# State reads head by head, in two column halves of TensorE, with the column sums directly behind

## The chip, the cores and the metric

The kernel runs on one core of a Trainium2 chip. The core has engines with a queue of instructions each: TensorE (PE) multiplies matrices, VectorE (DVE), ScalarE (ACT) and GpSimd (POOL) work on tiles element by element, SyncE (SP) issues DMAs. SBUF is the working memory with 128 partitions; PSUM takes TensorE's results in eight banks. The metric is the time of one execution on the device in microseconds (us), the median of several runs; lower is better.

A matmul of TensorE has a stationary operand, the weights, which a separate instruction (LDWEIGHTS, row PEld of the profile) loads into the array, and a moving operand that streams through it. In the profile "128\*64 128x32" would be weights of 128 rows and 64 columns, and a moving operand of 128 partitions and 32 columns.

## The reference

Inputs are `x` (8 batches, 8 heads, 512 tokens, 64 features), `state` (8, 8, 32, 64) and the weights of a feed-forward layer. For each batch and head:

```
scores = x @ state^T / 8            # 512 x 32
xread  = softmax over the 32 states  of scores   @ state    # 512 x 64
sread  = softmax over the 512 tokens of scores^T @ x        #  32 x 64
rows   = concat(xread, sread)       # 544 rows a batch, heads side by side: 512 columns
h = rows @ w_in; g = h + sin(alpha*h)^2/alpha; out = g @ w_out
```

The change concerns `sread`, the state reads: for each head, the sum over tokens of exp(score) times x, and its denominator, the sum over tokens of exp(score).

## The kernel before

Each batch has 512 tokens in four chunks of 128 (`C` = 4), and eight heads as four pairs (`Q` = 4), two pairs to a group (`G` = 2). `E` holds the exponentials of a batch: 128 tokens by group, chunk, and 128 columns, which are two pairs by two heads by 32 states (`Ns`). `xp` holds x with tokens on the partitions: chunk, head, 64 features.

The order of all instructions is written out by hand in the list `ORDER` (line 21 on): each word is a step with its arguments, and since every engine works through its own instructions in that order, the list sets each engine's queue. The steps that matter here:

- `sc`, `ex` (scores, exponentials of a group), `rs`, `rr`, `nm`, `ad` (the softmax over states and its transposed copy).
- `w.b.bank` (line 445): the reads of batch b. For each pair and chunk, one matmul with both heads of x as weights (128 tokens x 128 columns) and both heads' exponentials moving (64 columns). The four chunks accumulate in PSUM. The result has heads (even features, odd features) on the partitions and (even states, odd states) on the columns; only the two diagonal blocks, even with even and odd with odd, are used by anybody.
- `cs.b` (line 456): the denominators. Weights are a tile of ones, 128 x 64; for each chunk one matmul for the even heads into PSUM partitions 0 to 63 and one for the odd heads into 64 to 127, 128 moving columns each, into the last third of the same PSUM tile. `half(r)` (line 203) is the slice of 64 partitions.
- `rc.b` (line 466): DVE takes the reciprocal of the sums. `xs.b.r` (line 470): DVE multiplies the block of parity r on partition half r with it, and writes `xs_all`, which the feed-forward of "batch 8", all state rows together, uses late.
- `m` (line 478): the state times w_in for a later batch, in matmuls with 64 x 32 weights.
- `h`, `si`, `sq`, `gt`, `o`, `oc`, `os`: the feed-forward in 16 slices of 128 hidden columns. `h` (line 537) and `o` (line 587) are the bulk of TensorE's work, with 128 x 128 weights and 512 moving columns.

In the list `w.0`, `w.2` and `w.4` stand some steps ahead of their `cs`, with o or h steps between. `cs.0` and `cs.2` stand directly before an `m` as TensorE sees it. `w.1`, `w.3`, `w.6`, `w.7` are followed by their `cs` with no other TensorE work between. `w.5` comes before `w.7`, and `cs.5` directly behind `cs.7`.

Of the kernel before, what the change touches and what calls it, by code (L numbers as in the profile page):

```python
# [56 lines left out]
o.1.1.4.7 sq.1.11.A pk.3.0.V sq.1.14.G o.1.1.7.8 gt.1.10 td.3 o.1.2.8.9 sc.2.0.0 o.1.1.8.9 gt.1.11  # L57
o.1.1.9.10 ex.2.0 o.1.3.0.2.6 gt.1.14 o.1.3.2.4 o.1.2.9.10 o.1.3.4.5 o.1.2.10.12 ex.2.1 o.1.2.12.13
rs.2.0 o.1.1.10.11 m.2.2.2.4.3.0 rr.2.0 rs.2.1 o.1.2.13.14 nm.2.0.0.4.G me.2.3.0.A o.1.2.14.15 w.0.1
rr.2.1 me.2.2.1.A me.2.3.1.V o.1.3.5.6 nm.2.1.0.4.G me.2.2.0.A o.1.3.6.7 o.1.2.15.16 cs.0 oc.1.2.A  # L60
m.2.0.3.4.0.2 ad.2 rc.0 o.1.3.7.8 me.2.1.1.A o.1.3.8.9 sc.3.0.7 xs.0.1 me.2.1.0.A o.1.1.11.12 os.1.2
me.2.0.0.V sc.3.1.2 me.2.0.1.A o.1.1.12.13 o.1.3.9.10 xs.0.0 o.1.3.10.11 ex.3.0 o.1.1.13.16 ex.3.1
rs.3.0 o.1.3.11.13 oc.1.1.A o.1.3.13.14 rr.3.0 h.2.0.0 rs.3.1 nm.3.0.0.4.G os.1.1 o.1.3.14.16 si.2.0
# [28 lines left out]
sq.4.1.G gt.4.2 o.3.3.12.13 h.4.13.6 si.4.3 gt.4.15 o.3.3.13.15 si.4.13 sq.4.3.G o.3.3.15.16 gt.4.1  # L92
h.4.6.5 oc.3.3.A o.3.2.12.13 h.4.5.1 sq.4.13.G si.4.6 gt.4.3 os.3.3 h.4.14.2 si.4.5 o.3.0.0.1.4
sq.4.6.G o.3.2.13.14 gt.4.13 si.4.14 o.3.0.1.4 sq.4.5.A h.4.4.0 sq.4.14.G gt.4.6 o.3.0.4.5 h.4.0.6
si.4.4 gt.4.5 o.3.1.4.6 si.4.0 sq.4.4.G gt.4.14 o.3.2.14.16 w.2.5 sq.4.0.A pk.6.1.V o.3.1.6.7
oc.3.2.A h.4.7.1 pk.6.0.V gt.4.4 sc.5.0.2 td.6 si.4.7 o.3.1.7.8 sc.5.1.7 gt.4.0 o.3.1.8.9 o.3.0.5.6
ex.5.0 sq.4.7.G o.3.0.6.8 o.3.1.9.11 os.3.2 o.3.0.8.9 gt.4.7 o.3.0.9.12 cs.2 ex.5.1 rs.5.0
m.5.0.0.6.1.2 o.3.0.12.13 rr.5.0 me.5.0.0.A rs.5.1 o.4.3.0.1.7 nm.5.0.0.4.G o.3.0.13.14 me.5.0.1.A
o.3.0.14.15 rr.5.1 o.3.1.11.12 me.5.1.1.V o.3.1.12.13 me.5.1.0.A nm.5.1.0.4.G o.4.3.1.3 rc.2
o.3.0.15.16 o.4.3.3.4 o.3.1.13.14 oc.3.0.A ad.5 o.3.1.14.15 xs.2.0 m.6.0.0.6.2.1 xs.2.1 o.4.3.4.5  # L100
me.6.1.1.V me.6.1.0.A sc.6.1.4 os.3.0 sc.6.0.5 me.6.0.1.A o.4.3.5.6 me.6.0.0.V o.4.3.6.7 ex.6.0
o.4.3.7.8 o.4.0.0.1.2 o.3.1.15.16 ex.6.1 rs.6.0 w.3.1 oc.3.1.A cs.3 rr.6.0 m.5.2.6.0.5.4 rs.6.1
nm.6.0.0.4.G os.3.1 o.4.3.8.9 me.5.2.0.A me.5.2.1.V o.4.0.1.2 o.4.3.9.10 me.5.3.0.A o.4.3.10.11
rr.6.1 o.4.2.0.1.3 rc.3 nm.6.1.0.4.G o.4.2.1.2 me.5.3.1.A h.5.8.6 o.4.3.11.12 xs.3.1 h.5.9.0 si.5.8
ad.6 xs.3.0 o.4.0.2.3 o.4.3.12.14 o.4.2.2.4 h.5.4.5 si.5.9 o.4.3.14.15 sq.5.8.V h.5.3.4 si.5.4
gt.5.8 o.4.2.4.5 sq.5.9.G h.5.0.1 si.5.3 o.4.3.15.16 o.4.0.3.4 si.5.0 sq.5.4.G o.4.2.5.6 oc.4.3.V
o.4.2.6.8 sq.5.3.A gt.5.9 h.5.1.6 os.4.3 sq.5.0.G h.5.5.7 gt.5.4 si.5.1 o.4.2.8.10 si.5.5 gt.5.3
h.5.2.0 sq.5.1.G o.4.2.10.11 gt.5.0 o.4.2.11.12 si.5.2 h.5.14.5 lx.7.0.1 sq.5.5.A gt.5.1 h.6.3.4
o.4.2.12.13 si.5.14 gt.5.5 o.4.2.13.14 sq.5.2.G o.4.0.4.5 o.5.0.0.1.1 si.6.3 o.4.2.14.15 h.6.6.6
sq.5.14.A sq.6.3.G gt.5.2 o.4.0.5.6 h.5.13.7 si.6.6 gt.5.14 o.4.0.6.8 si.5.13 sq.6.6.G o.4.0.8.9  # L110
gt.6.3 o.4.0.9.11 sq.5.13.A o.4.0.11.12 h.6.2.0 gt.6.6 h.5.12.5 si.6.2 gt.5.13 o.4.2.15.16 h.6.4.4
si.5.12 sq.6.2.G o.4.0.12.13 oc.4.2.V o.4.0.13.14 si.6.4 o.4.0.14.15 o.4.1.0.1.6 os.4.2 o.4.1.1.2
sq.5.12.A gt.6.2 sq.6.4.G o.5.0.1.3 o.4.0.15.16 gt.5.12 h.5.10.7 oc.4.0.A o.4.1.2.3 gt.6.4 o.4.1.3.4
si.5.10 o.4.1.4.5 os.4.0 o.4.1.5.6 pk.7.1.V o.4.1.6.7 sq.5.10.A o.4.1.7.8 pk.7.0.V o.4.1.8.10 td.7
gt.5.10 m.6.2.3.0.5.2 o.4.1.10.11 me.6.3.0.V me.6.3.1.A o.4.1.11.12 h.5.7.4 me.6.2.1.A me.6.2.0.V
h.5.11.7 si.5.7 h.5.15.2 si.5.11 h.5.6.5 sq.5.7.V h.6.15.0 si.5.15 gt.5.7 sq.5.11.G o.4.1.12.13
o.5.2.0.1.3 si.5.6 o.5.2.1.3 si.6.15 sq.5.15.G o.4.1.13.14 gt.5.11 o.4.1.14.16 sq.5.6.A h.6.11.4
sq.6.15.G oc.4.1.V h.6.1.7 si.6.11 gt.5.15 o.5.2.3.4 os.4.1 h.6.0.6 si.6.1 sq.6.11.G gt.5.6
o.5.0.3.5 si.6.0 o.5.0.5.6 w.4.2 sq.6.1.A gt.6.15 sq.6.0.G o.5.0.6.7 gt.6.11 o.5.0.7.8 o.5.2.4.5
sc.7.1.5 gt.6.1 sc.7.0.0 o.5.2.5.7 ex.7.0 gt.6.0 o.5.0.8.10 o.5.2.7.8 o.5.1.0.2.4 o.5.0.10.11  # L120
h.6.14.7 ex.7.1 h.6.13.6 rs.7.0 cs.4 si.6.14 rs.7.1 o.5.1.2.4 o.5.0.11.12 rr.7.1 o.5.0.12.13 rc.4
o.5.2.8.9 nm.7.1.0.4.G h.6.10.0 o.5.0.13.14 si.6.13 xs.4.1 o.5.2.9.10 sq.6.14.G o.5.2.10.11 xs.4.0
si.6.10 o.5.2.11.13 h.6.7.5 sq.6.13.A rr.7.0 nm.7.0.0.4.G o.5.2.13.15 si.6.7 h.6.12.2 sq.6.10.A
gt.6.14 gt.6.13 o.5.1.4.5 ad.7 sq.6.7.G o.5.1.5.7 si.6.12 gt.6.10 o.5.1.7.10 sq.6.12.A gt.6.7
o.5.1.10.11 o.5.0.14.15 o.5.1.11.12 gt.6.12 o.5.0.15.16 h.6.5.7 oc.5.0.A o.6.2.0.1.6 h.6.9.0 si.6.5
os.5.0 o.5.2.15.16 o.5.1.12.13 si.6.9 sq.6.5.V o.5.1.13.14 o.6.2.1.2 oc.5.2.V o.5.3.0.1.5 sq.6.9.A
o.6.2.2.3 o.5.3.1.2 gt.6.5 os.5.2 o.6.2.3.5 o.5.3.2.3 gt.6.9 o.5.3.3.7 m.7.2.2.1.3.7 o.5.1.14.15
me.7.3.0.A me.7.3.1.V o.6.2.5.7 me.7.2.0.A o.6.2.7.8 me.7.2.1.V w.6.0 cs.6 m.7.0.3.7.2.1 rc.6
o.5.3.7.8 me.7.1.0.A o.5.3.8.10 me.7.0.1.V me.7.0.0.A o.5.3.10.11 h.6.8.2 me.7.1.1.A xs.6.0
o.5.3.11.12 xs.6.1 h.7.11.3 si.6.8 o.5.3.12.13 h.7.7.7 si.7.11 sq.6.8.V o.5.1.15.16 gt.6.8 w.5.1  # L130
si.7.7 sq.7.11.G o.5.3.13.14 oc.5.1.A o.6.3.0.1.0 o.5.3.14.15 sq.7.7.A o.5.3.15.16 gt.7.11 os.5.1
h.7.0.2 oc.5.3.A w.7.4 gt.7.7 si.7.0 cs.7 os.5.3 cs.5 h.7.5.3 rc.7 sq.7.0.A o.6.3.1.3 si.7.5
h.7.15.5 xs.7.0 xs.7.1 o.6.3.3.4 sq.7.5.A rc.5 o.6.3.4.6 o.6.2.8.9 si.7.15 o.6.2.9.11 gt.7.5
o.6.3.6.7 sq.7.15.A o.6.3.7.8 h.7.3.7 gt.7.0 o.6.3.8.9 h.7.14.4 si.7.3 gt.7.15 h.7.8.3 si.7.14
xs.5.0 sq.7.3.G h.7.6.2 xs.5.1 si.7.8 o.6.3.9.10 o.6.2.11.13 sq.7.14.G si.7.6 gt.7.3 o.6.2.13.16
# [22 lines left out]
class Steps:  # L158
# [245 lines left out]
    def ex(k, b, g):  # L404
        E = k.new(b, "E", k.epool, [k.P, k.G, k.C, k.P], BF16)
        k.nc.scalar.activation(E[:, g], k.t["sc", b, g][:], ACT.Exp, scale=k.scale)  # L406

    def rs(k, b, g):
        R = k.new(b, "R", k.smallp, [k.P, k.G, k.C * 4], FP32)
        k.nc.vector.reduce_sum(  # L410
            R[:, g], k.t["E", b][:, g].rearrange("p c (h j) -> p (c h) j", j=k.Ns), axis=AX.X
        )
# [5 lines left out]
    def nm(k, b, g, c0, c1, eng):  # L418
        A = k.new(b, "A", k.apool, [k.P, k.G, k.C, k.P], BF16)
        n = (c1 - c0) * 2  # L420
        a = A[:, g, c0:c1].rearrange("p c (e r j) -> p (c e) r j", r=2, j=k.Ns)
        e = k.t["E", b][:, g, c0:c1].rearrange("p c (e r j) -> p (c e) r j", r=2, j=k.Ns)
        rb = k.t["rR", b][:, g, c0 * 4:c1 * 4].rearrange("p (e r) -> p e r", r=2)
# [20 lines left out]

    def w(k, b, bank):
        wc = k.t["w", b] = k.ps(bank, [k.P, k.Q, 3 * k.Ns], FP32, "w_ps")
        E = k.t["E", b]
        for q in range(k.Q):
            for i in range(k.C):
                k.nc.tensor.matmul(  # L450
                    wc[:, q, 0:2 * k.Ns], k.pair(b, i, q),
                    E[:, q // 2, i, (q % 2) * 2 * k.Ns:(q % 2 + 1) * 2 * k.Ns],
                    start=(i == 0), stop=(i == k.C - 1),
                )

    def cs(k, b):
        E, wc = k.t["E", b], k.t["w", b]
        for i in range(k.C):
            for r in range(2):
                Ev = E[:, :, i, :].rearrange("p g (h r j) -> p g h r j", h=2, r=2)  # L460
                k.nc.tensor.matmul(  # L461
                    wc[k.half(r), :, 2 * k.Ns:], k.ones[:], Ev[:, :, :, r],
                    start=(i == 0), stop=(i == k.C - 1),
                )
# [199 lines left out]
```

The softmax here doesn't subtract the row's maximum and nothing guards it: scores larger than these inputs give would overflow.

## Time and profile before

| | us |
|---|---|
| median of 3 runs (221.13 to 221.43) | 221.16 |
| span of the profiled execution | 221.2 |
| TensorE busy | 215.7 |
| ScalarE busy | 173.5 |
| VectorE busy | 162.4 |
| GpSimd busy | 107.1 |
| reads `w` (line 450), 128 matmuls, busy | 5.0 |
| sums `cs` (line 461), 64 matmuls, busy | 3.1 |
| `m` (line 488), 256 matmuls, busy | 10.2 |

TensorE's granted clock is shown as full for the whole span. Busy times of TensorE overlap each other at their ends, because a matmul's length as shown includes the tail in which the next one already runs. What a matmul costs in a stream is the distance from its start to the next one's. "idle before <-issue" on a row of PEld is time in which the weight loader waited for nothing that the profile shows. The trace holds every start to a nanosecond; its views print hundredths of a microsecond.

### The profile page before, as it was taken

How to read it: one execution, taken by the hardware profiler on the slowest of the kernel's cores; microseconds unless marked ns; L12 is line 12 of the kernel's file. 1: busy time of each engine (PE TensorE's matmuls, PEld its weight loads, DVE VectorE, ACT ScalarE, POOL GpSimd, SP SyncE). 2: the span in 40 equal slices, each digit the busy share in tenths (PEclk: the TensorE clock that was granted, in tenths of full speed). 3: DMA queues.
4: the chain of work that ended last, by engine and by line, in shares of the span. 5: the costliest groups of instructions: out<-in, count | busy, mean ns of one | idle time of the engine just before them, and what ended most of it. 6: DMA issues, size and time to landing. Idle time of an engine off the chain costs nothing.

```text
span 221.2 us, 4330 instructions
## 1 busy us (share of the span) xinstructions
PE 215.7 (97%) x1619; PEld 106.0 (48%) x1619; DVE 162.4 (73%) x286; ACT 173.5 (78%) x297; POOL 107.1 (48%) x115
## 2 busy tenths in 40 slices
PE   7999999999999999999999999999999999999994
PEld 3664454444444444444454444445445555665452
DVE  3468986999678979988888778889766988571201
ACT  3589878998899979998996999798857897685111
POOL 6866626595388728934863377363501072121000
PEclk9999999999999999999999999999999999999999
DMA  6999995953549518375325437380220211012042
GB/s 172 198 206 204 205 203 87 174 199 73 119 127 158 96 50 150 44 190 61 81 41 125 126 95 94 108 117 17 47 99 0 98 47 47 0 50 95 1 142 96
DMA packets 38052, 23.48 MB, mean 106 GB/s; under 512 B 20992, under 2 KB 33680, under 8 KB 38032
## 3 DMA queue, kind: packets, MB, share of 16 engines
q0 software_dynamic: 11648, 8.13, 26.1%
q1 hardware_dynamic: 26128, 15.08, 26.1%
q8 instruction: 12, 0.20, 0.4%
q14 instruction: 8, 0.07, 0.1%
q10 hardware_dynamic: 256, 0.01, 0.1%
HBM read 17.44 MB, written 8.91 MB: 119 GB/s over the span
## 4 chain that ended last, share of the span: by engine, by line
PE 93%; ACT 3%; DMA 2%; SPq 0%; issue 0%
PE o_ps L587 54%; PE h_ps L537 22%; PE m_ps L488 4%; PE h_ps L543 3%; PE h_ps L552 3%; DMA x<-in_x_dram 2%; PE s_ps L399 2%; PE warm_ps L303 2%; PE w_ps L450 2%; PE w_ps L461 1%; PE x_ps L361 1%; ACT L226 1%; ACT s L560 1%; ACT M L496 1%; PE x_ps L376 0%; PE st_ps L333 0%
## 5 line engine op out<-in xcount | busy, mean ns | idle before, releaser
L587 PE MATMUL o_ps<-w_out_sb,gT 128*128 128x512 bf16 (+2 forms) x560 | 137.7, 373 | 0.0
L576 DVE SCALAR_TENSOR_TENSOR gT<-s,inva_sb,h_ps 128x512 bf16<-128x512 bf16 (+1 forms) x144 | 96.6, 714 | 18.8 <-POOL s L201 9.6
L201 POOL TENSOR_TENSOR s<-s 128x512 bf16<-128x512 bf16 (+1 forms) x76 | 76.7, 1021 | 65.9 <-ACT s L560 62.4
L560 ACT ACTIVATE s<-h_ps,alpha_sb 128x512 bf16<-128x512 f32 (+1 forms) x144 | 88.8, 671 | 10.5 <-PE h_ps L543 4.3
L587 PEld LDWEIGHTS <-gT 128*128 128x128 bf16 x560 | 52.3, 98 | 60.3 <-issue 5.0
L537 PE MATMUL h_ps<-AT,M 128*128 128x512 bf16 x224 | 60.8, 379 | 0.0
L537 PEld LDWEIGHTS <-M 128*128 128x128 bf16 x224 | 21.7, 98 | 25.9 <-issue 0.4
L569 ACT ACTIVATE s<-s 128x512 bf16<-128x512 bf16 (+1 forms) x53 | 31.4, 595 | 0.8
L201 POOL TENSOR_TENSOR A<-E,rR 128x512 bf16<-128x512 bf16 x16 | 16.6, 1048 | 25.7 <-ACT o_sb L595 12.7
L595 ACT COPY o_sb<-o_ps 128x512 f32<-128x512 f32 (+2 forms) x24 | 13.7, 571 | 16.6 <-PE o_ps L587 16.5
L496 ACT CAST M<-m_ps 128x512 bf16<-128x512 f32 x35 | 18.6, 594 | 8.2 <-PE m_ps L488 8.1
L496 DVE CAST M<-m_ps 128x512 bf16<-128x512 f32 x29 | 18.9, 679 | 2.5 <-PE m_ps L488 2.1
L595 DVE COPY o_sb<-o_ps 128x512 f32<-128x512 f32 x11 | 7.6, 691 | 13.0 <-PE o_ps L587 12.9
L303 PE MATMUL warm_ps<-warm 128*128 128x128 bf16 (+3 forms) x66 | 9.9, 295 | 1.4 <-DVE warm L209 1.2
L410 DVE TENSOR_REDUCE R<-E 128x16 f32<-128x512 bf16 x16 | 10.4, 658 | 1.1 <-ACT E L406 0.9
L201 DVE TENSOR_TENSOR s<-s 128x512 bf16<-128x512 bf16 (+1 forms) x15 | 6.2, 415 | 6.8 <-ACT s L560 6.7
L488 PE MATMUL m_ps<-w_in_sb,stT 64*32 64x512 bf16 x256 | 10.2, 382 | 0.0
L468 DVE RECIPROCAL rC<-w_ps 128x128 f32<-128x128 f32 x8 | 7.6, 948 | 3.2 <-PE w_ps L461 3.2
L406 ACT ACTIVATE E<-s_ps 128x512 bf16<-128x512 f32 x16 | 8.8, 601 | 1.4 <-PE s_ps L399 1.3
L552 PE MATMUL h_ps<-AT,M 128*128 128x512 bf16 x32 | 9.4, 380 | 0.4 <-ACT M L496 0.4
L543 PE MATMUL h_ps<-xs_all,w_in_sb 128*128 128x256 bf16 x64 | 9.1, 273 | 0.0
L560 ACT ACT_TABLE_LOAD x5 | 6.4, 1283 | 2.2 <-PE h_ps L537 1.1
(56 smaller groups left out, 104.3 us busy)
## 6 DMA issues: line engine op xcount, KB each, us to landing
out_dram<-o_sb SPq DMA_DIRECT2D x33, 256.0 KB, 2.3
xnat<-in_x_dram POOLq DMA_DIRECT2D x7, 512.0 KB, 7.7
w_in_sb<-in_moe_w_in_dram POOLq DMA_DIRECT2D x4, 512.0 KB, 10.3
w_out_sb<-in_moe_w_out_dram POOLq DMA_DIRECT2D x4, 512.0 KB, 16.3
x<-in_x_dram SPq DMA_DIRECT2D x4, 256.0 KB, 4.3
st_nat<-in_state_dram POOLq DMA_DIRECT2D x1, 256.0 KB, 5.7
out_dram<-o_sb SPq DMA_DIRECT2D x1, 192.0 KB, 1.9
s<-in_state_dram SPq DMA_DIRECT2D x1, 128.0 KB, 2.1
```

What stands on the lines that cost most here:

```text
L201: {"V": k.nc.vector, "G": k.nc.gpsimd}[eng].tensor_tensor(out, a, b, ALU.mult)
L303: k.nc.tensor.matmul(wp[:, :cols], k.warm[:, 0:k.P], k.warm[:, :cols], start=True, stop=True)
L488: k.nc.tensor.matmul(k.t["m", b, s + n, g][o0:o0 + k.Ns, :], k.stT[k.half(r), b * k.G + g, c0:c0 + k.Ns], k.w_in_sb[k.half(r), 2 * g + h, ...
L496: k.copy(eng)(k.t["M", b][:, g, s * k.FW:(s + 1) * k.FW], k.t["m", b, s, g][:])
L537: k.nc.tensor.matmul(hp[:, :n], k.t["M", t][:, g, fs], k.t["AT", t][:, g, :], start=(g == 0), stop=(g == k.G - 1),)
L543: k.nc.tensor.matmul(hp[:, :n], k.w_in_sb[:, q, fs], k.xs_all[:, q].rearrange("p b j -> p (b j)"), start=(q == 0), stop=(q == k.Q - 1),)
L552: k.nc.tensor.matmul(k.t["h", t, f][:], k.t["M", t][:, g, f * k.P:(f + 1) * k.P], k.t["AT", t][:, g, :], start=(g == 0), stop=(g == k.G - 1),)
L560: k.nc.scalar.activation(s[:, :n], k.t["h", t, f][:, :n], ACT.Sin, scale=k.alpha_sb[:, f:f + 1])
L569: k.nc.scalar.activation(s2[:, :n], s[:, :n], ACT.Square)
L576: k.nc.vector.scalar_tensor_tensor(gT[:, :n], k.t["s2", t, f][:, :n], k.inva_sb[:, f:f + 1], k.t["h", t, f][:, :n], ALU.mult, ALU.add,)
L587: k.nc.tensor.matmul(k.t["o", t, st, half][:, cols], k.t["gT", t, f][:, rows], k.w_out_sb[:, f, cols], start=(f == 0), stop=(f == k.FT - 1),)
L595: k.copy(eng)(o_sb[:, cols], k.t["o", t, st, half][:, cols])
```

## The change

`w` takes head after head. For each pair, chunk and parity r it issues one matmul with that head's 64 features as weights and that head's 32 exponential columns moving, and writes the diagonal block alone: partitions 64r to 64r + 63, columns 32r to 32r + 31 of the pair's part of the tile. The blocks off the diagonal are no longer computed. The number of matmuls in `w` goes from 16 to 32 a batch. In the list every `cs.b` moves to stand directly behind `w.b`.

```diff
     def w(k, b, bank):
         wc = k.t["w", b] = k.ps(bank, [k.P, k.Q, 3 * k.Ns], FP32, "w_ps")
-        E = k.t["E", b]
+        xp, E = k.t["xp", b], k.t["E", b]
         for q in range(k.Q):
             for i in range(k.C):
-                k.nc.tensor.matmul(
-                    wc[:, q, 0:2 * k.Ns], k.pair(b, i, q),
-                    E[:, q // 2, i, (q % 2) * 2 * k.Ns:(q % 2 + 1) * 2 * k.Ns],
-                    start=(i == 0), stop=(i == k.C - 1),
-                )
+                for r in range(2):
+                    c = (q % 2 * 2 + r) * k.Ns
+                    k.nc.tensor.matmul(
+                        wc[k.half(r), q, r * k.Ns:(r + 1) * k.Ns],
+                        xp[:, i, 2 * q + r, :], E[:, q // 2, i, c:c + k.Ns],
+                        start=(i == 0), stop=(i == k.C - 1),
+                    )
```

In the list of steps, as far as TensorE's order goes (other engines' steps left out):

```
before                                        after
w.0.1  o o o  cs.0  m.2.0                     w.0.1  cs.0  o o o  m.2.0
w.1.2  cs.1                                   w.1.2  cs.1
w.2.5  h, sc.5, o ...  cs.2  m.5.0            w.2.5  cs.2  h, sc.5, o ...  m.5.0
w.3.1  cs.3  m.5.2                            w.3.1  cs.3  m.5.2
w.4.2  o, sc.7, h ...  cs.4                   w.4.2  cs.4  o, sc.7, h ...
w.6.0  cs.6  m.7.0                            w.6.0  cs.6  m.7.0
w.5.1  ...  w.7.4  cs.7  cs.5                 w.5.1  cs.5  ...  w.7.4  cs.7
```

More of the change, by code (lines that the diff above doesn't have):

```diff
@@ L59 @@
 rs.2.0 o.1.1.10.11 m.2.2.2.4.3.0 rr.2.0 rs.2.1 o.1.2.13.14 nm.2.0.0.4.G me.2.3.0.A o.1.2.14.15 w.0.1
-rr.2.1 me.2.2.1.A me.2.3.1.V o.1.3.5.6 nm.2.1.0.4.G me.2.2.0.A o.1.3.6.7 o.1.2.15.16 cs.0 oc.1.2.A
+cs.0 rr.2.1 me.2.2.1.A me.2.3.1.V o.1.3.5.6 nm.2.1.0.4.G me.2.2.0.A o.1.3.6.7 o.1.2.15.16 oc.1.2.A
 m.2.0.3.4.0.2 ad.2 rc.0 o.1.3.7.8 me.2.1.1.A o.1.3.8.9 sc.3.0.7 xs.0.1 me.2.1.0.A o.1.1.11.12 os.1.2
@@ L94 @@
 sq.4.6.G o.3.2.13.14 gt.4.13 si.4.14 o.3.0.1.4 sq.4.5.A h.4.4.0 sq.4.14.G gt.4.6 o.3.0.4.5 h.4.0.6
-si.4.4 gt.4.5 o.3.1.4.6 si.4.0 sq.4.4.G gt.4.14 o.3.2.14.16 w.2.5 sq.4.0.A pk.6.1.V o.3.1.6.7
+si.4.4 gt.4.5 o.3.1.4.6 si.4.0 sq.4.4.G gt.4.14 o.3.2.14.16 w.2.5 cs.2 sq.4.0.A pk.6.1.V o.3.1.6.7
 oc.3.2.A h.4.7.1 pk.6.0.V gt.4.4 sc.5.0.2 td.6 si.4.7 o.3.1.7.8 sc.5.1.7 gt.4.0 o.3.1.8.9 o.3.0.5.6
-ex.5.0 sq.4.7.G o.3.0.6.8 o.3.1.9.11 os.3.2 o.3.0.8.9 gt.4.7 o.3.0.9.12 cs.2 ex.5.1 rs.5.0
-m.5.0.0.6.1.2 o.3.0.12.13 rr.5.0 me.5.0.0.A rs.5.1 o.4.3.0.1.7 nm.5.0.0.4.G o.3.0.13.14 me.5.0.1.A
@@ L99 @@
[L99 to L126, printed above, removed]
+ex.5.0 sq.4.7.G o.3.0.6.8 o.3.1.9.11 os.3.2 o.3.0.8.9 gt.4.7 o.3.0.9.12 ex.5.1 rs.5.0 m.5.0.0.6.1.2
@@ new lines @@
+o.3.0.12.13 rr.5.0 me.5.0.0.A rs.5.1 o.4.3.0.1.7 nm.5.0.0.4.G o.3.0.13.14 me.5.0.1.A o.3.0.14.15
+rr.5.1 o.3.1.11.12 me.5.1.1.V o.3.1.12.13 me.5.1.0.A nm.5.1.0.4.G o.4.3.1.3 rc.2 o.3.0.15.16
+o.4.3.3.4 o.3.1.13.14 oc.3.0.A ad.5 o.3.1.14.15 xs.2.0 m.6.0.0.6.2.1 xs.2.1 o.4.3.4.5 me.6.1.1.V
+me.6.1.0.A sc.6.1.4 os.3.0 sc.6.0.5 me.6.0.1.A o.4.3.5.6 me.6.0.0.V o.4.3.6.7 ex.6.0 o.4.3.7.8
+o.4.0.0.1.2 o.3.1.15.16 ex.6.1 rs.6.0 w.3.1 cs.3 oc.3.1.A rr.6.0 m.5.2.6.0.5.4 rs.6.1 nm.6.0.0.4.G
+os.3.1 o.4.3.8.9 me.5.2.0.A me.5.2.1.V o.4.0.1.2 o.4.3.9.10 me.5.3.0.A o.4.3.10.11 rr.6.1
@@ new lines @@
+o.4.2.0.1.3 rc.3 nm.6.1.0.4.G o.4.2.1.2 me.5.3.1.A h.5.8.6 o.4.3.11.12 xs.3.1 h.5.9.0 si.5.8 ad.6
+xs.3.0 o.4.0.2.3 o.4.3.12.14 o.4.2.2.4 h.5.4.5 si.5.9 o.4.3.14.15 sq.5.8.V h.5.3.4 si.5.4 gt.5.8
+o.4.2.4.5 sq.5.9.G h.5.0.1 si.5.3 o.4.3.15.16 o.4.0.3.4 si.5.0 sq.5.4.G o.4.2.5.6 oc.4.3.V o.4.2.6.8
+sq.5.3.A gt.5.9 h.5.1.6 os.4.3 sq.5.0.G h.5.5.7 gt.5.4 si.5.1 o.4.2.8.10 si.5.5 gt.5.3 h.5.2.0
+sq.5.1.G o.4.2.10.11 gt.5.0 o.4.2.11.12 si.5.2 h.5.14.5 lx.7.0.1 sq.5.5.A gt.5.1 h.6.3.4 o.4.2.12.13
+si.5.14 gt.5.5 o.4.2.13.14 sq.5.2.G o.4.0.4.5 o.5.0.0.1.1 si.6.3 o.4.2.14.15 h.6.6.6 sq.5.14.A
@@ new lines @@
+sq.6.3.G gt.5.2 o.4.0.5.6 h.5.13.7 si.6.6 gt.5.14 o.4.0.6.8 si.5.13 sq.6.6.G o.4.0.8.9 gt.6.3
+o.4.0.9.11 sq.5.13.A o.4.0.11.12 h.6.2.0 gt.6.6 h.5.12.5 si.6.2 gt.5.13 o.4.2.15.16 h.6.4.4 si.5.12
+sq.6.2.G o.4.0.12.13 oc.4.2.V o.4.0.13.14 si.6.4 o.4.0.14.15 o.4.1.0.1.6 os.4.2 o.4.1.1.2 sq.5.12.A
+gt.6.2 sq.6.4.G o.5.0.1.3 o.4.0.15.16 gt.5.12 h.5.10.7 oc.4.0.A o.4.1.2.3 gt.6.4 o.4.1.3.4 si.5.10
+o.4.1.4.5 os.4.0 o.4.1.5.6 pk.7.1.V o.4.1.6.7 sq.5.10.A o.4.1.7.8 pk.7.0.V o.4.1.8.10 td.7 gt.5.10
+m.6.2.3.0.5.2 o.4.1.10.11 me.6.3.0.V me.6.3.1.A o.4.1.11.12 h.5.7.4 me.6.2.1.A me.6.2.0.V h.5.11.7
@@ new lines @@
+si.5.7 h.5.15.2 si.5.11 h.5.6.5 sq.5.7.V h.6.15.0 si.5.15 gt.5.7 sq.5.11.G o.4.1.12.13 o.5.2.0.1.3
+si.5.6 o.5.2.1.3 si.6.15 sq.5.15.G o.4.1.13.14 gt.5.11 o.4.1.14.16 sq.5.6.A h.6.11.4 sq.6.15.G
+oc.4.1.V h.6.1.7 si.6.11 gt.5.15 o.5.2.3.4 os.4.1 h.6.0.6 si.6.1 sq.6.11.G gt.5.6 o.5.0.3.5 si.6.0
+o.5.0.5.6 w.4.2 cs.4 sq.6.1.A gt.6.15 sq.6.0.G o.5.0.6.7 gt.6.11 o.5.0.7.8 o.5.2.4.5 sc.7.1.5 gt.6.1
+sc.7.0.0 o.5.2.5.7 ex.7.0 gt.6.0 o.5.0.8.10 o.5.2.7.8 o.5.1.0.2.4 o.5.0.10.11 h.6.14.7 ex.7.1
+h.6.13.6 rs.7.0 si.6.14 rs.7.1 o.5.1.2.4 o.5.0.11.12 rr.7.1 o.5.0.12.13 rc.4 o.5.2.8.9 nm.7.1.0.4.G
@@ L127 @@
+h.6.10.0 o.5.0.13.14 si.6.13 xs.4.1 o.5.2.9.10 sq.6.14.G o.5.2.10.11 xs.4.0 si.6.10 o.5.2.11.13
+h.6.7.5 sq.6.13.A rr.7.0 nm.7.0.0.4.G o.5.2.13.15 si.6.7 h.6.12.2 sq.6.10.A gt.6.14 gt.6.13
+o.5.1.4.5 ad.7 sq.6.7.G o.5.1.5.7 si.6.12 gt.6.10 o.5.1.7.10 sq.6.12.A gt.6.7 o.5.1.10.11
+o.5.0.14.15 o.5.1.11.12 gt.6.12 o.5.0.15.16 h.6.5.7 oc.5.0.A o.6.2.0.1.6 h.6.9.0 si.6.5 os.5.0
+o.5.2.15.16 o.5.1.12.13 si.6.9 sq.6.5.V o.5.1.13.14 o.6.2.1.2 oc.5.2.V o.5.3.0.1.5 sq.6.9.A
 o.6.2.2.3 o.5.3.1.2 gt.6.5 os.5.2 o.6.2.3.5 o.5.3.2.3 gt.6.9 o.5.3.3.7 m.7.2.2.1.3.7 o.5.1.14.15
@@ L130 @@
 o.5.3.11.12 xs.6.1 h.7.11.3 si.6.8 o.5.3.12.13 h.7.7.7 si.7.11 sq.6.8.V o.5.1.15.16 gt.6.8 w.5.1
-si.7.7 sq.7.11.G o.5.3.13.14 oc.5.1.A o.6.3.0.1.0 o.5.3.14.15 sq.7.7.A o.5.3.15.16 gt.7.11 os.5.1
-h.7.0.2 oc.5.3.A w.7.4 gt.7.7 si.7.0 cs.7 os.5.3 cs.5 h.7.5.3 rc.7 sq.7.0.A o.6.3.1.3 si.7.5
+cs.5 si.7.7 sq.7.11.G o.5.3.13.14 oc.5.1.A o.6.3.0.1.0 o.5.3.14.15 sq.7.7.A o.5.3.15.16 gt.7.11
+os.5.1 h.7.0.2 oc.5.3.A w.7.4 cs.7 gt.7.7 si.7.0 os.5.3 h.7.5.3 rc.7 sq.7.0.A o.6.3.1.3 si.7.5
 h.7.15.5 xs.7.0 xs.7.1 o.6.3.3.4 sq.7.5.A rc.5 o.6.3.4.6 o.6.2.8.9 si.7.15 o.6.2.9.11 gt.7.5
```

## The prediction

> **What bounds the kernel now.** I read three views in this order: the busy shares, TensorE's waits, and the timeline of TensorE around the two steps that change.
>
> ```profile
> PE 215.7 (97%) x1619; PEld 106.0 (48%) x1619; DVE 162.4 (73%) x286; ACT 173.5 (78%) x297; POOL 107.1 (48%) x115
> ...
> PE   7999999999999999999999999999999999999994
> ```
>
> A modelled busy share says little by itself, so the waits of TensorE come next. These are all of them:
>
> ```profile
> PE warm_ps L303 <- DVE warm L209: 1.2, 1, 1.2
> PE x_ps L361 <- ACT xp L356: 0.5, 1, 0.5
> PE h_ps L552 <- ACT M L496: 0.4, 1, 0.4
> PE warm_ps L303 <- ACT M L496: 0.2, 1, 0.2
> ```
>
> Four waits, 2.3 us, on lines 303, 361 and 552, which belong to the warm-up and to batch 0. From about 20 us to the last matmul at 217.9 us TensorE waits for nobody: consecutive 512-column matmuls start 216 ns apart, and every longer step between starts is at a change of tile shape (but for one of 0.1 us at 29.8 us). So time added to or taken from TensorE in this stretch moves the end one for one, and nothing of it lies beside other work. DVE, ACT and POOL wait for TensorE or for each other and are not the limit.
>
> The timeline of TensorE for batch 0 (start, length, line, shape, count):
>
> ```profile
> 55.82 0.60 PE L587 MATMUL o_ps<-w_out_sb,gT 128*128 128x512 bf16 x2
> 56.26 0.63 PE L450 MATMUL w_ps<-E,xp 128*128 128x64 bf16 x16
> 56.72 0.81 PE L587 MATMUL o_ps<-w_out_sb,gT 128*128 128x512 bf16 x3
> 57.47 0.41 PE L461 MATMUL w_ps<-E,ones 128*64 128x128 bf16 x8
> 57.81 0.63 PE L488 MATMUL m_ps<-w_in_sb,stT 64*32 64x512 bf16 x16
> 58.37 0.39 PE L587 MATMUL o_ps<-w_out_sb,gT 128*128 128x512 bf16 x1
> ```
>
> Lengths of TensorE rows include a modelled pipeline tail; the cost is in the starts. The read step `w` holds TensorE from 56.26 to 56.72 us: 0.46 us for 16 matmuls, 29.2 ns each by the trace's nanosecond starts. The column sums `cs` hold it from 57.47 to 57.81. Their 8 matmuls run as 4 pairs, one in each half of the array's columns: the two of a pair start 3 to 4 ns apart, and pairs follow each other every 55.8 ns.
>
> A change of shape costs a bubble. The last 512-column matmul before `cs` starts 309 ns ahead of it and not 216 (+93); the first weights are then loaded in the open (+24: the second pair starts 80 ns after the first). On the way back the next matmul starts 152 ns after the last sum and not 56 (+96), and its successor after 226 ns and not 216 (+10). A round trip to half-columns is 93 + 24 + 96 + 10 = 223 ns. `cs` alone between two o steps so costs 448 ns (310 + 195 + 149 between its neighbours becomes 654 with the way back, less 216, plus 10). Directly before `m`, whose shape needs the same two changes anyway, it costs 344.
>
> **Two rules of the Trainium skill.** "TensorEngine Tiling (Array Packing)", section Key Properties, says that a change of tiling mode drains the engine while tiles of one mode run side by side. The rows above agree: 93 to 96 ns a change, 3 to 4 ns between the two of a pair. "TensorE: Matmul & The Clock Gate", section LDWEIGHTS, puts a weight load at its columns over 1.2 GHz, which for 64 columns is an estimate of 53 ns; the tiling page adds that column tiling switches the fast load off. The trace has two answers to that:
>
> ```profile
> 57.46 0.11 PEld L461 LDWEIGHTS <-ones 128*64 128x64 bf16 x2 [0.42 <-issue]
> ```
> ```profile
> 57.49 0.17 PEld L461 LDWEIGHTS <-ones 128*64 128x64 bf16 x4
> ```
>
> The first pair of loads starts at 57.464 us and the second pair, into the same halves, at 57.492: 28 ns later (28 or 29 at the other places with this shape, on lines 333, 376 and 461). The full 128x128 load after `m` is followed by the next one 15 ns later. In the steady stream of `cs` the loads never show: 55.8 ns is also the distance of 128-column matmuls with full weights, so there the moving columns set the pace. I go by the 28 ns, not by the page's 53.
>
> **The change part by part.**
>
> 1. Removed: 8 x 16 reads with 128 weight columns and 64 moving, 29.2 ns each, 3.74 us in all, half of whose products nobody reads.
>
> 2. Added: 8 x 32 reads with 64 weight columns and 32 moving, in 8 x 16 pairs. The price of a pair, p, is not in the trace; all else is. Moving columns: 128 take 55.8 and 64 take 29.2, so 32 take 29.2 - 26.6/2 = 15.9 ns. Weights: the next load starts 1.7 ns after the matmul that uses the last one, and from there to the matmul's effective start 26 ns pass (2 + 24 above), so 27.7; the measured load to load is 28 to 29. p is the larger. Bounds: 15.9 from below (loads hidden) and 55.8 from above (a load as dear as the page says; `cs` shows that it is no dearer). I take 28.5. That makes 128 x 28.5 = 3.65 us, against 3.74 removed: -0.09 us.
>
> 3. Moved: `cs` goes directly behind `w`. `w` now has the shape of `cs`, so the change that before lay between them (124 ns in place of 29 where they were adjacent) lies ahead of `w`. By batch:
>    - 1, 3 and 6 were adjacent already, and 4 had both between full-shape matmuls: the number of changes stays. 0 ns but for roundings of at most 4.
>    - 0 and 2 had `cs` directly before `m` and shared its changes. `cs` now returns to full shape and `m` pays for itself: 448 - 344 = 104 ns each.
>    - 5 had `cs` directly behind `cs` of batch 7 and cost only 4 x 55.8 = 223 ns (16 sums there take 418 from first to last, 8 take 195). Now it has its own round trip: about +221 ns.
>    Sum: 104 + 104 + 221 = +0.43 us, four more one-way changes of shape.
>
> 4. Queues and waits: no DMA, no work of DVE, ACT or POOL is added or moved. `cs` needs the exponentials that `w` has already needed, and writes the bank that `w` already holds, so it brings no new wait. The reciprocal `rc` (line 468) waits 3.2 us for `cs` in all; DVE sees `cs` earlier, which is worth nothing since TensorE waits for no one. Between the new and the old place of `cs` the o and h steps run about 0.45 us later, which gives their producers slack. Bank releases to `m` do not move ahead of TensorE.
>
> 5. Instructions: 16 more matmuls and 16 more loads a batch. The queue hands out 32 of them in 0.25 us in `m`, so 80 in 0.7 us is no faster; but in `m` they may have stood in the queue. Cost 0 to 0.5 us; I take 0, since 32 transposes (line 376), 4 o, 16 scores and 8 `m` run from 27.6 to 30.2 us with no step but those of shape and one of 0.1 us.
>
> Sum: -0.09 + 0.43 = +0.34 us, or as a formula **128 p - 3.31 us** with p in us. The profiled span is 221.2 us (221.185), the median of the runs 221.16: the span stands for the runs to 0.03 us, and the runs lie 0.3 us apart. 221.16 + 0.34 = **221.5 us**, +0.15%, which is inside the 0.2% (0.44 us) that a measurement of this kernel can tell from no change.
>
> **The rivals.**
> - Slower by weight loads. If a 64-column load can't be hidden behind 32 moving columns and takes 53 to 56 ns, p is 55.8: +3.8 us, 225.0. For it: the page's figure, and no row here has weights wider than the moving side in this shape. Against: loads 28 ns apart. It decides from p = 29.3 on, where +0.44 is passed; that is only 0.8 ns above my value. A middle form, loads of the two halves hindering each other or a few ns of handshake each, has p from 29.3 to 42: +0.45 to +2.1, typically 222.2.
> - Slower by instruction supply: the 0 to 0.5 us of step 5 on top of the forecast, up to 222.0.
> - Faster: loads overlap fully and p is 15.9: -1.27 us, 219.9. It needs p below 22.4. Against: no second load into a half before 28 ns.
> - The change doesn't do what it says: even and odd heads do not run side by side. Then a pair is two singles of 28 ns, the time of the first rival. Against: every pair of `cs` starts within 4 ns.
>
> **How the numbers follow.** Forecast 0.54 (own range 221.2 to 221.6); middle form 0.20; full weight-load rival, with the failing pairs, 0.12; instruction supply 0.09; faster 0.05. Slower takes 0.20 + 0.12 + 0.09 = 0.41, same 0.54, faster 0.05. The range runs from 221.1 to 223.0: it holds the forecast, the supply rival and the middle form nearly whole, and leaves out the far ends 219.9 and 225.0, 0.17 together.
>
> **What would show it.** In the timeline after: pairs of `w` every 28 to 29 ns; `w` with `cs` one block of 0.66 us from first to last start; 309 ns ahead of `w`, then no bubble between `w` and `cs`, 152 ns behind; `m` of batches 2 and 5 (behind the reads of 0 and 2) entered from a full shape. TensorE's waits stay the four above. The prediction is wrong if the pairs of `w` stand over 30 ns apart, if steps appear inside the block that no shape explains, or if TensorE waits for DVE or ACT after 20 us.

## The result and the profile after

The changed kernel takes 223.74 us (median of 6 runs, 223.04 to 225.30), the kernel before 221.21 us (6 runs, 221.13 to 221.43): a ratio of 1.0107, 95% interval 1.0075 to 1.0139, or 1.7 to 3.1 us more. The forecast was no measurable change, at 221.5.

TensorE's waits in the profile after, all of them:

```profile
PE s_ps L399 <- DMA xT<-xp: 1.5, 1, 1.5
PE warm_ps L303 <- DVE warm L209: 1.2, 1, 1.2
PE h_ps L554 <- ACT M L498: 0.4, 1, 0.4
PE warm_ps L303 <- ACT M L498: 0.2, 1, 0.2
```

The first row is new. The scores of batch 4 (line 399) wait for the transposed copy of x (`xT`, the DMA of step `td.4`, line 389). The timeline of TensorE there:

```profile
74.22 1.03 PE L589 MATMUL o_ps<-w_out_sb,gT 128*128 128x512 bf16 x4
76.75 0.64 PE L399 MATMUL s_ps<-stT,xT 128*128 128x64 bf16 x16 [1.50 <-DMA xT<-xp]
```

The same scores in the kernel before:

```profile
75.68 1.46 PE L587 MATMUL o_ps<-w_out_sb,gT 128*128 128x512 bf16 x6
76.97 0.63 PE L399 MATMUL s_ps<-stT,xT 128*128 128x64 bf16 x16
```

After the change the last `o` matmul starts at 74.87 us and the scores at 76.75: 1.88 us where it was 0.22 before, so 1.66 us are lost. None of this touches the reads or the sums. The reads themselves, batch 0 (timeline of TensorE):

```profile
54.32 0.68 PE L452 MATMUL w_ps<-E,xp 128*64 128x32 bf16 x32
54.84 0.39 PE L463 MATMUL w_ps<-E,ones 128*64 128x128 bf16 x8
55.17 0.82 PE L589 MATMUL o_ps<-w_out_sb,gT 128*128 128x512 bf16 x3
```

32 matmuls take 0.53 us up to the sums, without a bubble between the two. By the nanosecond starts the pairs stand 31.7 ns apart behind the first (0, 53, 85, 116, 148, 180 ns and so on), the step before `w` is 309 ns, the step behind `cs` 152.

Where the DMAs stand in this stretch answers why the copy is late. These are the queues in three windows of the profile after, 73.50 to 74.65, 74.65 to 74.75 and 75.3 to 76.8 us (queue: packets, MB, share of 16 engines):

```profile
q1 hardware_dynamic: 799, 0.20, 92.7%
```
```profile
q8 instruction: 1, 0.02, 60.5%
q1 hardware_dynamic: 3, 0.00, 3.4%
```
```profile
q1 hardware_dynamic: 2, 0.00, 0.2%
```

The data packets of the copy (queue 1) end at 74.708 us. At 74.704 one packet of queue 8 starts: 16,384 bytes of program code, 0.97 us long. The copy's semaphore counts 16 increments, and by the trace 15 of them arrive by 75.15 us and the last at 76.70. The two last packets of the copy, 4 bytes each, which I take for its increments (32 such packets, two for each of the 16), run at 75.66 and 75.67, as the code packet ends; the other thirty ran by 74.55. So some 1.1 us of the delay lie ahead of these two packets. The increment itself follows them after 1.03 us where the others took 0.6; these 0.4 us the trace doesn't explain. For comparison, in the kernel before all 16 increments of this copy fall within 0.15 us (76.68 to 76.83), and the code packet comes at 77.9 us, when these scores are over (76.97 to 77.44).

The program got one code packet more, which the page of each kernel shows (before, then after):

```profile
q8 instruction: 12, 0.20, 0.4%
```
```profile
q8 instruction: 13, 0.21, 0.4%
```

The trace has 3,238 matmuls and weight loads of TensorE before and 3,494 after: 256 more, which is one packet by the size that the section named next gives. Before, the packet started 1.17 us behind the start of the last `o` matmul ahead of the scores of batch 4; after, 0.17 us ahead of it. My reading, which the experiments test, is that the 32 more instructions of `w.0` bring this fetch forward, into the end of the copy.

The Trainium skill has rules that bear on this in two places. "Runtime: NRT & Kernel Launch", section Instruction fetch mechanics: code comes in blocks of 16 KiB or 256 instructions, which the sequencer fetches over a DMA queue of its own while it executes. That agrees with the packets. It adds that the cost is mostly hidden; here TensorE is never seen to run short of code, but the packet is not hidden from other DMAs. "DMA: Bandwidth & Descriptors", section Queues, rings and completion order: a semaphore's increment lands only after every earlier write of that DMA engine, across its queues. That fits 15 punctual increments and one late one. Which of the 16 engines carried which packet no record here shows.

One reading of the profile before was wrong, though no difference hangs on it. The page's span, 221.2 us, is not the time of the run: in all other runs of both kernels about 1.9 us lie outside the span (after: 223.49 us with a span of 221.6; before: 221.21 with 219.3). The profiled execution of before was a late starter; it reached its first state transposes (line 333) at 10.99 us, the other ten profiled executions of this case at 8.6 to 9.4. I therefore compare traces by the stretch from the first of those transposes to the start of the last matmul: 206.89 us before, 209.31 after, **+2.43 us**.

### The profile page after: what moved, and what is told of

Read it like the earlier page. It is cut to its first block, busy times and chain, and to the rows that moved or that the text cites. A ratio compares the mean times of both kernels' runs of the same rounds, so it can differ in the third digit from the quotient of the medians.

```text
span 221.6 us, 4586 instructions
## 1 busy us (share of the span) xinstructions
PE 215.1 (97%) x1747; PEld 104.4 (47%) x1747; DVE 162.5 (73%) x286; ACT 173.4 (78%) x297; POOL 106.9 (48%) x115
## 4 chain that ended last, share of the span: by engine, by line
PE 91%; DMA 4%; ACT 3%; SPq 0%; issue 0%
PE o_ps L589 52%; PE h_ps L539 21%; PE m_ps L490 4%; PE h_ps L545 3%; DMA xT<-xp 3%; PE h_ps L554 3%; PE w_ps L452 2%; PE s_ps L399 2%; DMA x<-in_x_dram 2%; PE warm_ps L303 1%; PE w_ps L463 1%; ACT L226 1%; ACT s L562 1%; ACT M L498 1%; PE x_ps L361 1%; PE st_ps L333 0%
## 5 line engine op out<-in xcount | busy, mean ns | idle before, releaser
L303 PE MATMUL warm_ps<-warm 128*128 128x128 bf16 (+3 forms) x66 | 9.0, 277 | 1.4 <-DVE warm L209 1.2
```

Source lines behind the costliest of these rows:

```text
L303: k.nc.tensor.matmul(wp[:, :cols], k.warm[:, 0:k.P], k.warm[:, :cols], start=True, stop=True)
```

## The experiments

Unless a run says otherwise, times stand against runs of the kernel before on the same chip: 221.33 us for the first four, 221.03 for the next three, 221.09 for the last two. "Stretch" is the one just defined, as a difference to before.

**The two halves of the change, apart.** In the first the reads are split and the list of steps is the old one (list of the changed kernel, then of this one, cut short):

```diff
-w.0.1 cs.0 ... w.2.5 cs.2 ... w.4.2 cs.4 ... w.5.1 cs.5
+w.0.1 ... cs.0 ... w.2.5 ... cs.2 ... w.4.2 ... cs.4 ... w.5.1 ... cs.5
```

> The reads split head by head, the column sums left at their old places. My account of TensorE's starts: where w and cs stand apart (batches 0, 2, 4, 5) w now pays its own way into half-columns and back, about 0.25 us each; where they are adjacent 0.04 us each: +1.2 us of TensorE time. The program has the same 32 more TensorE instructions ahead of the scores of batch 4 as the changed kernel, so by the theory of a code fetch that falls on the transposed copy of batch 4 the wait of 1.5 to 1.7 us at those scores appears too: +2.8 us, 224.0. By the rival that the wait comes from the moved column sums or from a chance of that one execution: +1.2 us, 222.4, and no wait at the scores of batch 4.

Measured: 224.33 us, ratio 1.0122 (1.0094 to 1.0151), stretch +3.12. The wait at the scores is there, 1.85 us by the starts. What is left, 1.27 us, is the forecast 1.2 for shapes and reads and a step of `h` at 72.0 us that takes 0.08 longer than before.

In the second the sums are moved and the reads are as before (reads of the changed kernel, then of this one, cut short):

```diff
-                        wc[k.half(r), q, r * k.Ns:(r + 1) * k.Ns], ...
+                    wc[:, q, 0:2 * k.Ns], k.pair(b, i, q), ...
```

> The reads as before with 128 weight columns, the column sums moved directly behind them. Four more one-way changes of shape: +0.43 us of TensorE time. No instruction is added, so by the code-fetch theory no wait at the scores of batch 4: 221.6. By the rival that the move makes the wait: 223.2.

Measured: 221.53 us, ratio 1.0006 (0.9990 to 1.0022), stretch +0.49, of which 0.04 is a short wait at the scores for a copy with all 16 increments together; the code packet comes at 76.2 us. So the moved sums cost what four changes of shape cost, and the wait comes with the split.

**Is it the split, or only the number of instructions?** The kernel before, its reads and sums untouched, with one warm-up cut into smaller pieces (3,588 columns for 3,584):

```diff
-... consts touch lq.0.S ident_ l_alpha lq.1.S zero.0 warm_up.7.512.3 exp_table ...
+... consts touch lq.0.S ident_ l_alpha lq.1.S zero.0 warm_up.23.156.3 exp_table ...
```

> The kernel before with nothing changed but its first warm-up: 23 matmuls of 156 columns in place of 7 of 512, the same number of columns and 32 more TensorE instructions at the very start. By the code-fetch theory the 16 KB of code that are fetched at 77.9 us before are asked for 32 instructions earlier, at about 74.5 us, into the transposed copy of batch 4: a wait of about 1.5 us at its scores, 222.8. By every rival that puts the wait on the reads or the sums: no wait, 221.2 (within 0.3).

Measured: 223.64 us, ratio 1.0106 (1.0076 to 1.0137), stretch +2.57. TensorE's waits in its profile:

```profile
PE s_ps L399 <- DMA xT<-xp: 1.6, 1, 1.6
PE warm_ps L303 <- DVE warm L209: 1.2, 1, 1.2
PE h_ps L537 <- DMA AT<-A: 0.7, 1, 0.7
```

The wait of the changed kernel appears at the same scores, with 15 increments by 75.63 us and the last at 77.18; by the starts it is 1.73 us. A second one of 0.84 us came that I had not foreseen, at the first `h` of batch 1, which needs the transposed copy of its attention (`AT`) at once. A code packet runs from 33.06 to 34.00 us, between the issue of this copy (32.70) and its first data packet (33.99). The pattern is another one: the data end at 35.65 us, in the usual time, and then all 16 increments come late, 1.3 to 1.8 us behind the data, where nine traces without a code packet at this place have 0.3 to 0.5. How the packet would do this is not shown. 1.73 + 0.84 = 2.57, the whole stretch. So 32 instructions that change no work at all cost this kernel what the whole change costs.

**Taking the wait out of the changed kernel.** Warm-ups are merged, with the same number of columns, so that fewer instructions stand ahead (the list, cut short):

```diff
-xc.0.1.0.A warm_up.1.256.3 xtq.3.2 warm_up.2.128.3 ex.0.0 warm_up.2.128.4 ...
+xc.0.1.0.A warm_up.1.256.3 xtq.3.2 warm_up.1.256.3 ex.0.0 warm_up.1.256.4 ...
```

Eight of them:

> The changed kernel with eight of its warm-ups as one matmul of 256 columns in place of two of 128: the same columns, 16 TensorE instructions fewer ahead of everything else. By the code-fetch theory the fetch that lay at 74.7 us comes 16 instructions later, behind the start of the scores of batch 4, and the wait goes: what is left is +0.43 us for four changes of shape and +0.34 us for the pairs of reads, 222.0. By the rivals the wait stays: 223.7.

A miss: 223.60 us, ratio 1.0084 (1.0051 to 1.0117), stretch +2.53, the wait still there with 1.61 us. The code packet had not moved against TensorE's work: it starts 0.21 us ahead of the last `o` matmul before the scores, and 0.17 ahead in the changed kernel. One of the six runs took 221.84 us, as if without the wait; it has no trace. So I went further, to eighteen merged warm-ups:

> The changed kernel with eighteen of its warm-ups as one matmul of 256 columns in place of two of 128: 36 TensorE instructions fewer ahead of everything, 4 fewer than the kernel before has ahead of the scores of batch 4. With 16 fewer the code fetch still came 0.2 us ahead of the end of TensorE's last step before these scores; with the 32 fewer that the kernel with only the sums moved has, it came at 76.2 us, 1.0 us behind their start, and there was no wait. By the code-fetch theory the fetch therefore lies behind the start of the scores, the 1.6 us wait is gone, and +0.43 us for shape changes and +0.34 for the pairs are left: 222.0 to 222.1. By the rival that the split itself makes the wait: 223.7.

Measured: 222.08 us, ratio 1.0042 (1.0029 to 1.0055), stretch +0.75. The timeline of TensorE at the scores of batch 4:

```profile
74.24 1.46 PE L589 MATMUL o_ps<-w_out_sb,gT 128*128 128x512 bf16 x6
75.53 0.63 PE L399 MATMUL s_ps<-stT,xT 128*128 128x64 bf16 x16
```

No wait; the code packet comes at 76.4 us. Against the changed kernel the stretch is 1.68 us shorter, which is the wait. Two single runs place the limit and try the other direction:

> The changed kernel with twelve of its warm-ups as one matmul of 256 columns in place of two of 128: 24 TensorE instructions fewer. With 16 fewer the fetch stood 0.2 us ahead of the last step before the scores of batch 4, with 36 fewer 0.9 us behind their start. If the fetch moves with the instructions, it lies inside the scores (about 75.5 us) and there is no wait: 222.1. If it is held at one place until a limit between 24 and 36 is passed, it still lies at about 75 us, with the wait: 223.7.

Measured: 221.46 us once, stretch +0.81, no wait; the packet starts 1.2 us behind the start of the last `o` matmul. (The time is only 0.37 us above its one reference run. This execution reached its first state transposes at 8.56 us, the earliest of all, so I go by the stretch.)

```diff
-zero.0 warm_up.7.512.3 exp_table
+zero.0 warm_up.23.156.3 exp_table
```

> The changed kernel with the warm-up of 7 matmuls of 512 columns as 23 of 156: 32 TensorE instructions more. If the fetch moves with the instructions, it comes about 3.5 us earlier, at 71.2 us, ahead of the packets of the transposed copy (from 71.9 us), and the wait at the scores of batch 4 goes; in the kernel before, the same 32 more made another wait of 0.8 us at the transposed copy of batch 1 (36.4 us), which may appear here: 222.0 to 222.9. If it stays at 74.7 us: 223.7 or more.

Measured: 222.71 us once, stretch +1.56. The packet comes at 69.7 us, ahead of the copy, and the wait at the scores is gone, while the other one is there, again with a code packet (33.7 to 34.6 us) at the beginning of that copy (TensorE's waits):

```profile
PE h_ps L539 <- DMA AT<-A: 0.6, 1, 0.6
```

By the starts it is 0.79 us, and 0.75 + 0.79 = 1.54 is the stretch. The wait at the scores of batch 4 thus comes and goes with the place of the code packet, in both directions and with unchanged reads and sums. In all eleven traces of this case it stands where the packet meets the end of this copy (four) and nowhere else. Without it the copy's own variation made TensorE wait 0.18 us at most.

**What sets the 31.7 ns of a pair.** Both runs are built on the kernel with 36 fewer. With the exponentials of both heads moving, so that the unused blocks are computed again:

```diff
-                        wc[k.half(r), q, r * k.Ns:(r + 1) * k.Ns],
-                        xp[:, i, 2 * q + r, :], E[:, q // 2, i, c:c + k.Ns],
+                        wc[k.half(r), q, 0:2 * k.Ns], xp[:, i, 2 * q + r, :],
+                        E[:, q // 2, i, (q % 2) * 2 * k.Ns:(q % 2 + 1) * 2 * k.Ns],
```

> The kernel with 36 instructions fewer, each read of one head with the 64 exponential columns of both heads of its pair moving, not 32 (the blocks off the diagonal are computed again and read by nobody). If the load of 64 weight columns sets the 31.7 ns from pair to pair, the distance stays at 31 to 32 ns. If the moving columns have a part in it, 32 more of them at 13.3 ns per 32 give 45 ns, and 1.7 us more in all.

The distance is 31.6 ns, and its rows of TensorE differ from those of the kernel that it is built on by nothing in the step from reads to sums (here, then there):

```profile
54.46 0.69 PE L452 MATMUL w_ps<-E,xp 128*64 128x64 bf16 x32
54.99 0.39 PE L463 MATMUL w_ps<-E,ones 128*64 128x128 bf16 x8
```
```profile
54.76 0.68 PE L452 MATMUL w_ps<-E,xp 128*64 128x32 bf16 x32
55.29 0.39 PE L463 MATMUL w_ps<-E,ones 128*64 128x128 bf16 x8
```

Twice the moving columns cost the reads nothing. The run took 222.14 us once, stretch +1.02, which is 0.27 more than the kernel it is built on, but elsewhere: 0.09 in the start-up, and 0.18 at the scores of batch 4, whose copy landed that much later, with no code packet near. So the pace is not set by the moving columns. What is left is the load of 64 weight columns, or a fixed cost of a load with its matmul; no run with fewer weight columns tells these two apart. The other run takes the even heads of a batch first and then the odd ones:

```diff
-        for q in range(k.Q):
-            for i in range(k.C):
-                for r in range(2):
+        for r in range(2):
+            for q in range(k.Q):
+                for i in range(k.C):
```

> The kernel with 36 instructions fewer, with all even heads of a batch first and then all odd heads, so that successive reads go to the same half of the array's columns. If the two of a pair really ran side by side, each single read now stands 28 to 30 ns from the next: 0.9 us in place of 0.5 for a batch, +3.1 to +3.6 us in all. If the pair was only two loads after each other, the reads stand 15 to 16 ns apart and the time stays.

Single reads in one half stand 31.6 ns apart, a batch takes 0.90 us from first to last and not 0.50, the run 225.15 us once, stretch +4.01. So the two of a pair do run side by side, a load with its matmul costs the same whether the other half works too, and the split without the pairing would have cost 3.3 us more.

## Why the prediction was wrong

- *TensorE is the bound and its time moves the end one for one*: right. The stretches of all runs add up from shapes, reads and waits to within 0.1 us or so, and behind the start-up no wait for DVE, ACT or POOL appears. But the waits at the scores were for a DMA, which the sentence left out.
- *Four more one-way changes of shape, +0.43 us* (step 3): right; +0.49 alone. The bubbles of 309 ahead and 152 behind were as read.
- *The price of a pair, p = 28.5 ns* (step 2): right in kind, wrong in size. The weight side sets it and not the moving columns, and pairs run side by side, but in a steady stream it takes 31.7 ns from one load to the next. I took the distance of the first two loads after a change of shape, 28 ns, for the steady one. The changed kernel has the same start: its first three pairs of loads stand 28 ns apart, the following ones 31.7. The formula 128 p - 3.31 us gives +0.75 with 31.7, and the kernel without the wait has a stretch of +0.75. That is 0.4 us more than forecast, and enough to leave "no change" by itself: 1.0042 is outside 0.2%. The limit p = 29.3, which the prediction set for that, was passed, and 31.7 lies in the range of the middle rival. Of its two forms the halves do not hinder each other (31.6 ns alone, 31.7 together); a few ns more for each load fit.
- *The skill's 53 ns for a load of 64 columns* ("TensorE: Matmul & The Clock Gate", section LDWEIGHTS): no run here shows it; 31.7 is the measured distance. Going by the trace and not by the page was right, but its first pair was too small a sample.
- *Queues and waits: no DMA is added* (step 4): this is the step that failed in sense. The kernel's own DMAs are the same, but 256 more instructions are a DMA too: 13 code packets in place of 12, and those behind the first reads at other times.
- *Instructions, 0 to 0.5 us, taken at 0* (step 5): the failed step in size. I asked only whether TensorE's queue could be fed fast enough. It could; the cost was 1.66 us at another place, where the code packet held up the last increment of a copy that TensorE was about to need. The upper bound of 0.5 had no row behind it, and so the range's end of 223.0 lay too low.
- *TensorE's waits stay the four*: wrong. The one at batch 0's x copy (line 361) was gone in this execution, and the one at line 399 came. The signs of being wrong named DVE and ACT, and not a DMA.

In sum: 0.43 for shapes, 0.32 for reads and 1.66 for the wait are 2.41 us; the stretch shows 2.43 and the medians 2.53. The profile before did hold a warning. Its scores of batch 4 started at 76.97 us with the last increment of their copy at 76.83: the copy was 0.15 us ahead, with next to no slack.

What stays open is the exact rule by which the code packet's time follows the instructions. With 0 and 16 fewer instructions it stood at the same place against TensorE's work; with 24 fewer it was 1.4 us later, and stayed there with 36. The traces give the packet two places. In the four with the long wait it starts 4 ns before the copy's last data packet ends, however many instructions stand ahead. This looks as if it had been asked for earlier and had stood behind the data. In six of the seven others (the kernel before, only the sums moved, 24 and 36 fewer, and the two built on 36 fewer) it starts 1.00 to 1.15 us behind the copy's last increment. This looks as if it was asked for only when that increment had released TensorE. Both are readings from times, and no run tests them, but they would explain why 16 fewer moved nothing and 24 fewer moved 1.4 us.

Nor is nearness in time enough. At another copy of x, near 42 us, a code packet starts 15, 38 and 237 ns before the data end (in the last two runs above and in the one that they are built on), and all 16 increments are punctual. The only other late increment of these traces, by 1.56 us, is in the last run at 124.7 us, where nobody waited for it; there the packet again starts 4 ns before the data end.

## What to carry to other kernels

When a change adds instructions, count the program's code as DMA traffic: look where the packets of the instruction queue stand, and which copies that an engine is waiting for lie beside them. A copy whose last increment arrives just as it is needed has no room for a packet of a microsecond. Before a difference of one per cent is put down to the changed code, shift the program by a few dozen harmless instructions and see if the difference survives: here two thirds of it did not. And take the price of a repeated operation from the steady part of a stream, not from its first two members.

## What was not expected of the hardware

- A 16 KB code packet takes 0.9 to 2.0 us of DMA time here, and one that starts in the last nanoseconds of a copy's data can delay one of the copy's 16 increments by 1.5 us (75.15 to 76.70 us).
- In the half-column shape a load of 64 weight columns with its matmul has a price of 31.7 ns in a stream, in one half or in both at once, with 32 or 64 columns moving. Full 128x128 weights with 64 moving columns go at 29.2 ns. The narrower load is not cheaper.
- When all even heads are taken first, the first odd read starts 89 ns ahead of the last even one, and the first sum 89 ns ahead of the last read: by the trace, work for one half starts ahead of earlier work for the other.
